# A fused attention and gated-MLP layer on one core: every product moved onto the two 64-row halves of the array

## The chip, the cores and the metric

One of the eight cores of a Trainium2 chip runs the whole layer. The time is the device time of one execution, in microseconds (us). TensorE (PE) does the matmuls and writes their sums to PSUM, which has eight banks of 512 float32 columns on 128 partitions; ScalarE (ACT), VectorE (DVE) and GpSimd (POOL) do the rest; SyncE (SP) issues all transfers. Every engine works through its own list of instructions in order, and the lists meet in semaphores.

## The reference

`x` is 2048 tokens by 448. 16 heads of 28; each query sees 8 keys, 2 tokens apart, itself the last.

```python
h  = x + A(layernorm(x));  h2 = h + B(layernorm(h))

def A(x, wqkv, wo):                       # 16 heads, Dh = 28
    q, k, v = split(x @ wqkv)
    logits = einsum('bhsd,bhswd->bhsw', q, k[:, :, s - 2*w]) * Dh**-0.5   # w = 0..7
    return (softmax(logits) @ v[:, :, s - 2*w]) @ wo

def B(x, w_in, w_sp, b_sp, w_out):
    z  = gelu(x @ w_in)                   # 448 -> 2 * 896
    z1, z2 = z[..., :896], layernorm(z[..., 896:])
    g  = einsum('ts,bsf->btf', w_sp, z2) + b_sp[None, :, None]            # 2048 x 2048
    return (z1 * g) @ w_out
```

## The kernel before, in words

Python builds a list of jobs, each with an engine, an estimated duration, what it reads and writes, and how many PSUM banks it takes. A planner (`Planner.order`) lays them out in simulated time; where several jobs of an engine are ready it takes the one with the lowest number in `PRIO`, a list with one rank per job. The result fixes each engine's order of instructions. Semaphore waits are then derived from the reads and writes (`Sched.issue`); PE never waits for itself, because its matmuls end in order. `ON` says which engine a PSUM evacuation or copy runs on.

**Products.** The contraction is over 448 rows: three chunks of 128 and one of 64. `product` (L554) makes two PE jobs for one pair of PSUM banks. Job F: six matmuls over 128 rows, three for each bank. Job H: two matmuls over the last 64 rows, one for each bank; the data of that chunk lie twice, on partitions 0 to 63 and 64 to 127, so that one runs on the upper and one on the lower half of the array (`tile_position` (0, 0) and (64, 0)). All of these matmuls are recorded at L564. Products are:

- `qk{t}_{g}`: queries and keys, for six blocks of tokens `t` (128, 128, 256, 512, 512, 512 tokens) and four groups `g` of four heads. One bank gets q, the other k of those heads, 28 rows for each head in a strip of 32; four rows of each strip hold zeros. Evacuated by `qe{t}_{g}` into `qkT` (L581), even and odd tokens apart.
- `v{b}`: values, for two attention blocks at a time (nine jobs), evacuated by `ve{b}` into `V1` (L575).
- `y{m}`: the projection with `wo`, two blocks of 128 tokens (eight).
- `z2_{m}` (sixteen) and `z1_{u}` (fourteen): the two halves of `w_in`, tokens on the partitions for z2, features for z1.

**Attention.** 17 blocks of up to 128 queries. `lg{b}_{j}` (L874) makes the logits of eight heads, with 28-row matmuls on 32-row strips: `j` = 0 uses strips 0 and 1, `j` = 1 strips 2 and 3. `ex` (ACT, L883) takes the exponential, `mk` (DVE, L889) masks it, `o{b}` (PE, L898, 16 matmuls over 128 rows) multiplies with the values and sums, `rc` and `om` (DVE, L906 and L909) divide. Then a transposing transfer, a copy into `OT`, `y`, the sum with x `h` (DVE, L843), the second layer norm (L696, L698, L691, L707), and a transposing transfer into `hnT`. `E` has four slots, so `lg{b}` waits for `o{b-4}`.

**Gated MLP.** z2 and z1 wait for the last logits (`gate`), since the GELU (L965, L1010) and the exponential use different ACT tables. A z2 product with a non-zero entry in `RAW2` is exempt: it may run earlier, is copied out raw (L575), and gets its GELU in place (L962). Then statistics (L969, L972) and normalisation (L978), the spatial product `g` (L1043, 448 matmuls of 512 columns over 128 rows), the gate `ua`, `um` (L1051, L1054), the output product (L1066), the sum (L1073), the store. A matmul of PE with nothing to do at the start is a filler (L1081).

**Changes of row use.** The planner charges PE for a change between full (F), half (H) and logit (L) jobs: `SWITCH`, about 0.1 us each.

Of the kernel before, what the change touches and what calls it, by code (L numbers as in the profile page):

```python
# [5 lines left out]
S_TOK = 2048  # L6
D = 448
NHEAD = 16
DH = 28
# [10 lines left out]
SWITCH = {"FH": 0.096, "HF": 0.096, "FL": 0.1, "HL": 0.1, "LF": 0.03, "LH": 0.1}  # L20
# [4 lines left out]
LOOK = {'pe': 1e-09, 'act': 0.1762690089245428, 'dve': 0.17500524126766434, 'pool': 0.04342214756282488, 'sp':  # L25
        0.3037332826506372}
PRIO = [0, 3, 4, 5, 1, 2, 14, 9, 7, 6, 10, 8, 13, 12, 11, 50, 58, 41, 38, 63, 62, 40, 54, 0, 0, 7, 16, 22, 34, 21, 15,
# [34 lines left out]
KEY = dict(x=-10.145, xs=0.685, qk=-3.702, qkg=-1.064, v=-1.761, ve=-6.148, qe=-3.15, lg=-1.488, ex=5.497,  # L62
           mk=-3.215, o=2.696, om=0.603, oT=-1.054, hh=0.0, y=-5.759, h=0.564, ln2=4.478, hT=19.942, z2=74.834,
           z2s=0.028, zr=2.556, zrs=0.21, z1=34.42, z1s=2.041, g=84.462, gs=0.172, wo=1.509, wl=-9.273,
           wls=4.361, wp=-9.955)
WINB = 2
ON = {'xe0_0': 'dve', 'xe0_1': 'act', 'xe1_0': 'dve', 'nd0_9': 'dve', 'nd0_10': 'dve', 'wp0_0': 'act', 'wp0_1': 'act',
# [41 lines left out]
class Sched:  # L109
# [14 lines left out]
    def issue(self, exe, fn, reads=(), writes=(), dma=False):  # L124
# [23 lines left out]
        for e, c in sorted(needed.items(), key=lambda t: -t[1]):  # L148
# [8 lines left out]
            if c > myvc.get(e, 0):  # L157
                myvc[e] = c
# [980 lines left out]
```

## Time and profile before

| | us |
|---|---|
| three runs | 242.96, 242.97, 242.81 (median 242.96) |
| the profiled execution | 243.6 |
| its span, first to last instruction | 241.9 |
| last logits start (the group on `qkL`) | 73.2 |
| first spatial matmul | 109.2 |
| last start of a z2 group | 121.0 |

A row of a timeline gives the start, the time from the first start to the last end, engine, line, operation, tiles, rows by columns of the array used, the shape of the moving operand, and how many instructions were merged. Matmuls overlap by their fill and drain, so the spacing of their starts tells the price, not their duration. PEld is the load of weights, which runs under the matmuls. In a table of windows the columns are the window, its length, then PE, PEld, DVE, ACT and POOL, each with busy time and the number of instructions, the granted PE clock, the share of the transfer engines and GB/s. In a table of groups the numbers behind the bar are the busy time in us, the mean duration of one in ns, and, behind the second bar, the idle time before them and what ended it.

### The profile page before, as it was taken

How to read it: one execution, taken by the hardware profiler on the slowest of the kernel's cores; microseconds unless marked ns; L12 is line 12 of the kernel's file. 1: busy time of each engine (PE TensorE's matmuls, PEld its weight loads, DVE VectorE, ACT ScalarE, POOL GpSimd, SP SyncE). 2: the span in 40 equal slices, each digit the busy share in tenths (PEclk: the TensorE clock that was granted, in tenths of full speed). 3: DMA queues.
4: the chain of work that ended last, by engine and by line, in shares of the span. 5: the costliest groups of instructions: out<-in, count | busy, mean ns of one | idle time of the engine just before them, and what ended most of it. 6: DMA issues, size and time to landing. Idle time of an engine off the chain costs nothing.

```text
span 241.9 us, 4239 instructions
## 1 busy us (share of the span) xinstructions
PE 235.4 (97%) x1707; PEld 115.5 (48%) x1726; DVE 155.0 (64%) x319; ACT 92.6 (38%) x115; POOL 55.4 (23%) x110
## 2 busy tenths in 40 slices
PE   7999999999999999999999999999999999999995
PEld 5674545545545444444344444444444444434443
DVE  6999878998999999998573135106111920805554
ACT  2779777778989765666230000000000000033000
POOL 8535116255565533061111000000000000000000
PEclk9999999999999999999999999999999999999999
DMA  6954497958533999999899400000000020010112
GB/s 194 317 138 94 77 157 176 171 133 190 109 62 72 176 152 179 228 158 153 166 204 178 42 0 0 0 3 0 0 0 3 0 76 0 20 41 0 57 38 76
DMA packets 65923, 23.21 MB, mean 96 GB/s; under 512 B 58352, under 2 KB 65648, under 8 KB 65904
## 3 DMA queue, kind: packets, MB, share of 16 engines
q1 hardware_dynamic: 65904, 22.95, 46.9%
q8 instruction: 13, 0.21, 0.4%
q14 instruction: 6, 0.05, 0.1%
HBM read 6.83 MB, written 1.84 MB: 36 GB/s over the span
## 4 chain that ended last, share of the span: by engine, by line
PE 92%; DMA 2%; DVE 2%; SPq 1%; issue 1%; ACT 0%; ACTq 0%
PE psum L1043 40%; PE psum L564 37%; PE psum L1066 9%; PE psum L874 3%; PE psum L898 3%; DMA wraw<-in_A_wqkv_dram 2%; DVE E L889 1%; SPq L605 1%; DVE qkT L581 1%; ACT wqk L575 0%; PE psum L738 0%; DVE srg L1073 0%; PE psum L740 0%; ACTq L179 0%
## 5 line engine op out<-in xcount | busy, mean ns | idle before, releaser
L1051 DVE TENSOR_TENSOR ub<-psum,bb 128x512 bf16<-128x512 f32 x28 | 19.4, 691 | 50.4 <-PE psum L1043 50.0
L1043 PE MATMUL psum<-wsp_hi,z2p 128*128 128x512 bf16 x217 | 50.6, 379 | 0.4
L1010 ACT ACTIVATE z1p<-psum 128x1024 bf16<-128x1024 f32 x14 | 14.1, 1021 | 95.8 <-PE psum L564 95.8
L1043 PEld LDWEIGHTS psum<-wsp_hi,z2p 128*128 128x128 bf16 x224 | 21.8, 98 | 26.2 <-issue 0.4
L883 ACT ACTIVATE E<-psum 128x960 bf16<-128x960 f32 (+2 forms) x34 | 31.7, 973 | 6.5 <-PE psum L874 6.4
L564 PE MATMUL psum<-xhT,wqk 128*128 128x512 bf16 (+5 forms) x185 | 27.6, 306 | 1.0 <-issue 0.5
L1043 PE MATMUL psum<-wsp_la,z2p 128*128 128x512 bf16 x110 | 26.0, 379 | 0.1
L1043 PE MATMUL psum<-wsp_lb,z2p 128*128 128x512 bf16 x109 | 25.6, 379 | 0.2
L564 PE MATMUL psum<-w_in,hnT 128*128 128x448 bf16 (+1 forms) x128 | 24.3, 353 | 0.1
L564 PE MATMUL psum<-hnT,w_in 128*128 128x512 bf16 (+1 forms) x112 | 23.9, 379 | 0.0
L1066 PE MATMUL psum<-w_out,z1p 128*128 128x448 bf16 (+1 forms) x119 | 22.8, 341 | 0.0
L969 DVE BATCH_NORM_STATS2 st<-z2p 128x6 f32<-128x448 bf16 x32 | 19.2, 612 | 4.2 <-ACT z2p L965 3.7
L889 DVE TENSOR_TENSOR E<-E,maskb 128x1920 bf16<-128x1920 bf16 (+2 forms) x17 | 20.3, 1220 | 1.0 <-ACT E L883 1.0
L696 DVE BATCH_NORM_STATS2 st<-x_tm 128x6 f32<-128x448 bf16 x32 | 19.0, 612 | 1.5 <-DMA x_tm<-in_A_x_dram 1.3
L691 POOL TENSOR_TENSOR rs<-rs,negh 128x2 f32<-128x2 f32 (+2 forms) x22 | 18.6, 847 | 1.8
L564 PEld LDWEIGHTS psum<-xhT,wqk 128*128 128x128 bf16 (+1 forms) x192 | 12.6, 97 | 11.3 <-issue 3.2
L1043 PEld LDWEIGHTS psum<-wsp_la,z2p 128*128 128x128 bf16 x112 | 10.9, 98 | 13.3 <-issue 0.4
L1054 DVE TENSOR_TENSOR z1p<-ub,z1p 128x512 bf16<-128x512 bf16 x28 | 11.9, 424 | 8.4 <-ACT z1p L1010 7.5
L1043 PEld LDWEIGHTS psum<-wsp_lb,z2p 128*128 128x128 bf16 x112 | 11.0, 98 | 13.1
L581 ACT ACTIVATE qkT<-psum 128x1024 bf16<-128x1024 f32 (+2 forms) x22 | 15.0, 717 | 4.8 <-PE psum L564 4.5
L1066 PEld LDWEIGHTS psum<-w_out,z1p 128*128 128x128 bf16 x119 | 11.6, 98 | 10.3
L564 PEld LDWEIGHTS psum<-w_in,hnT 128*128 128x128 bf16 (+1 forms) x128 | 10.1, 97 | 12.7 <-issue 4.1
(63 smaller groups left out, 241.8 us busy)
## 6 DMA issues: line engine op xcount, KB each, us to landing
w_in<-in_B_w_in_dram SPq DMA_DIRECT2D x8, 224.0 KB, 3.2
out_dram<-srg SPq DMA_DIRECT2D x16, 112.0 KB, 1.7
x_tm<-in_A_x_dram SPq DMA_DIRECT2D x3, 448.0 KB, 6.2
w_out<-in_B_w_out_dram SPq DMA_DIRECT2D x1, 784.0 KB, 8.2
wraw<-in_A_wqkv_dram SPq DMA_DIRECT2D x1, 672.0 KB, 5.4
bb<-in_B_b_sp_dram SPq DMA_DIRECT2D x1, 512.0 KB, 6.4
wo<-in_A_wo_dram SPq DMA_DIRECT2D x1, 336.0 KB, 6.0
wv<-in_A_wqkv_dram SPq DMA_DIRECT2D x1, 336.0 KB, 6.2
```

Source lines behind the costliest of these rows:

```text
L564: ins = e.matmul(o, w, x, start=g not in seen, stop=left[g] == 0, **kw)
L581: return e.activation(o, i, AF.Copy) if eng == "act" else e.tensor_copy(o, i)
L691: (lambda e: e.tensor_tensor(R, A, negh[:, 0:1].to_broadcast([128, n]), ALU.pow), [rr, r_negh], r_rs[k][m:m + n])],
L696: [(lambda e: e.bn_stats(st[:, m, :], src), [rsrc], [r_st[k][m]])], dve_t(D))
L883: return e.activation(o, i, AF.Exp, scale=SCALE)
L889: return e.tensor_tensor(a, a, maskb[:, mi:mi + 1, pad:pad + nq].to_broadcast([NK, NHEAD, nq]), ALU.mult)
L969: [(lambda e, m=m, k=k: e.bn_stats(st3[:, m, k, :], z2p[:, m, D * k:D * (k + 1)]), [r_z2[m]], [r_st[2][m]])], dve_t(D))
L1010: return e.activation(o, i, AF.Gelu_apprx_tanh)
L1043: ins = e.matmul(psv(tk), z2p[:, s, 128 * fc:128 * fc + 128], w, start=(s == 0), stop=(s == NB - 1))
L1051: [(lambda e, tc=tc, s=s, tk=tk: e.tensor_tensor(ub[:, s, :], psv(tk), bb[:, 512 * tc:512 * tc + 512], ALU.add), [r_bb], [r_ub[s]])], dve_ ...
L1054: [(lambda e, fc=fc, tc=tc, s=s: e.tensor_tensor(z1p[:, fc, 512 * tc:512 * tc + 512], ub[:, s, :], z1p[:, fc, 512 * tc:512 * tc + 512], AL ...
L1066: ins = e.matmul(psv(tk, 0, c1 - c0), z1p[:, fc, 128 * m:128 * m + 128], w_out[:, fc, c0:c1], start=(fc == 0), stop=(fc == FC7 - 1))
```

## The change

- `product` makes two jobs of another cut. Job A: for each of the three 128-row chunks the upper 64 rows go to one bank and the lower 64 rows to the other; then the two matmuls of the last chunk, as before. Job B: the three chunks again with the banks exchanged. All are half-row matmuls, 14 for each product in place of six full and two half. As B's halves write the banks that A's other halves wrote, B's first instruction waits until PE's own semaphore has counted A (`own`, `behind`). Block 16's values, alone in one bank, become four full matmuls (`single`).
- From block `t` = 3 on (`T7`, tokens 512 to 2047) the product for the last four heads has only q. Their k comes from the four spare rows of each strip in the other seven banks: four POOL copies (`wr0` to `wr3`) put the weights there before block 3, `qs{t}` makes q in two banks of half the columns, and four transfers for each block (`qr{t}_{j}`, four more for `qkL`) gather the rows into the place of k. The logits wait for them.
- The planner learns the costs of the new kinds: the two logit jobs of a block are told apart by row half (L and M), a wait of B costs 0.25 us (`SELF`).
- `PRIO`, `ON`, `LOOK`, `KEY`, `WLH` and `GRES` are other; `RAW2` is all zeros. `OH` (the `o` jobs on halves) is off: `fo2` is not used.

```diff
-SWITCH = {"FH": 0.096, "HF": 0.096, "FL": 0.1, "HL": 0.1, "LF": 0.03, "LH": 0.1}
+SWITCH = {"FH": 0.111, "HF": 0.098}
+OH = False
+SELF = 0.25
...
-RAW2 = [0, 1, 2, 1, 1, 1, 1, 2, 1, 2, 1, 0, 0, 1, 0, 0]
+RAW2 = [0] * 16
 XEH = {0: 2}
-WLH = [4, 4, 8, 9, 18, 1, 4, 12, 24, 4, 14, 34, 6, 22, 21, 26]
-GRES = 1
+WLH = [2, 3, 5, 6, 8, 9, 11, 12]
+GRES = 4
...
-ON = {'xe0_0': 'dve', 'xe0_1': 'act', 'xe1_0': 'dve', 'nd0_9': 'dve', 'nd0_10': 'dve', 'wp0_0': 'act', 'wp0_1': 'act',
-      'wp1_0': 'act', 'wp4_0': 'act', 'wp4_1': 'act', 'qe4_1': 'dve', 'qe4_3': 'dve', 'oc1': 'pool', 've2': 'dve', 'od3':
-      'dve', 'oc3': 'pool', 've4': 'dve', 'od4': 'dve', 'oc5': 'pool', 'od6': 'dve', 'od7': 'dve', 'oc7': 'pool', 'nd1_5':
-      'dve', 've8': 'dve', 'oc9': 'pool', 've10': 'dve', 'oc11': 'pool', 'oc13': 'pool', 'nd1_10': 'dve', 'oc15': 'pool',
-      'nd1_14': 'dve', 'nd1_15': 'dve', 'z2c6': 'dve', 'z2c13': 'dve'}
+ON = {'xe0_1': 'act', 'nd0_8': 'dve', 'nd0_10': 'dve', 'nd0_13': 'dve', 'nd0_15': 'dve', 'wp0_0': 'act', 'wp1_1': 'act',
+      'wp2_0': 'act', 'wp2_1': 'act', 'wp3_0': 'act', 'wp4_0': 'act', 'wp4_1': 'act', 'qe0_1': 'dve', 'qe2_3': 'dve', 'qe3_0':
+      'dve', 'qe3_3': 'dve', 'qe4_0': 'dve', 'qe4_2': 'dve', 'qe5_0': 'dve', 've0': 'dve', 'oc1': 'pool', 've2': 'dve', 'oc3':
+      'pool', 'od5': 'dve', 'oc5': 'pool', 'oc7': 'pool', 'nd1_4': 'dve', 'od9': 'dve', 'oc9': 'pool', 'nd1_6': 'dve',
+      'nd1_7': 'dve', 'oc11': 'pool', 'od13': 'dve', 'od15': 'dve', 'oc15': 'pool', 'nd1_12': 'dve', 'nd1_15': 'dve'}
...
+        if own > myvc.get("own", 0):
+            waits.append((exe, own))
+            myvc["own"] = own
...
             def f(e, which):
-                parts = get()
...
-                for g, o, w, x, tp in parts[which]:
-                    left[g] -= 1
-                    kw = {} if tp is None else {"tile_position": tp}
-                    ins = e.matmul(o, w, x, start=g not in seen, stop=left[g] == 0, **kw)
-                    seen.add(g)
+                main, rest = get()
+                seqs = [[q for q in main if q[0] == k] for k in range(2)]
+                nc = len(seqs[0])
+                assert nc == len(seqs[1])
+                for c in range(nc):
+                    for k in range(2):
+                        g, o, w, x, _ = seqs[k ^ which][c]
+                        i = 64 * k
+                        ins = e.matmul(o, w[i:i + 64], x[i:i + 64], start=which == 0 and c == 0, stop=which == 1 and c == nc - 1,
+                                       tile_position=(i, 0))
+                if which == 0:
+                    for k, (g, o, w, x, tp) in enumerate(rest):
+                        assert g == k and tp == (64 * k, 0)
+                        ins = e.matmul(o, w, x, start=False, stop=False, tile_position=tp)
                 return ins
...
+            jh = pl.job(name + "B", "pe", key + KEY["hh"], [(lambda e: f(e, 1), reads, [])], half_t(n) * nc, acq=tk, kind="H")
+            jh.behind = jf
...
+            for i in range(4 if t == T7 else 0):
+                pool("wr%d" % i, KEY["wp"] + 20.0 + i, [
+                    (lambda e, i=i: e.tensor_copy(
+                        wqk[:, :, 0:7, :].rearrange("p c g (j q) -> p c g j q", q=32)[:, :, :, :, DH + i],
+                        wraw[:, :, D + 336:2 * D].rearrange("p c (j q) -> p c j q", q=28)[:, :, :, 7 * i:7 * i + 7].rearrange(
+                            "p c j g -> p c g j")), W_qk, [r_pad3[i]])], 0.5)
+            for g in range(3 if t >= T7 else 4):
...
+            product("qs%d" % t, key, f, [r_pad[6]] + r_pad2 + r_pad3 + xh_res(lo, hi), n // 2, 6, tk)
...
+            for j in range(4):
+                load("qr%d_%d" % (t, j), lambda j=j, lo=lo, hi=hi: qkv(slice(7, 8), lo, hi)[32 * j:32 * j + DH, 0],
+                     lambda j=j, lo=lo, hi=hi: qkT[32 * j + DH:32 * j + 32].rearrange("p g (r t) -> p (g r) t", r=2)[:, 0:14, lo // 2:hi // 2],
+                     [r_qr[t][j]], 0.6, (1.4, 0.2), key=lo / 112.0 + KEY["qe"] + 1.0, reads=r_qk[t])
```

More of the change, by code (lines that the diff above doesn't have):

```diff
@@ L79 @@
 LN1G = [(0, 1), (1, 1), (2, 2), (4, 4), (8, 4), (12, 4)]
+T7 = 3
 QT = [(0, 128), (128, 256), (256, 512), (512, 1024), (1024, 1536), (1536, 2048)]
@@ L122, in __init__, with issue @@
         self.store_keys = []
-    def issue(self, exe, fn, reads=(), writes=(), dma=False):
+    def issue(self, exe, fn, reads=(), writes=(), dma=False, own=0):
         prod, inc = exe, 1
@@ L197 @@
     __slots__ = ("eng", "key", "dur", "lat", "ops", "acq", "rel", "tick", "reserve",
-                 "deps", "ndep", "succ", "idx", "start", "end", "name", "tbl", "srv", "kind", "alts")
+                 "deps", "ndep", "succ", "idx", "start", "end", "name", "tbl", "srv", "kind", "alts", "behind", "done")
 class Planner:
@@ L219, in job @@
         j.alts = None
+        j.behind = None
+        j.done = 0
         deps = set(a for a in after if a is not None)
@@ L341, in order @@
             if e == "pe":
[L342 to L346 removed]
+                was, now = pstate[0], j.kind
+                if was.upper() in "LM" and now in "LM":
+                    if was.upper() != now and t < te[e] + 0.05:
+                        dur -= 0.1
+                        now = now.lower()
+                elif now in "LM":
+                    dur += 0.1
+                elif was in "LM":
+                    dur += 0.1
+                elif was in "lm":
+                    dur += 0.03
+                elif was != now:
+                    dur += SWITCH[was + now]
+                pstate[0] = now
             j.start = t
@@ L364, in order @@
                 s.ndep -= 1
-                a = j.end + (lat if s.eng != "pe" else 0.0 if e == "pe" else lat + FILL)
+                a = j.end + (lat if s.eng != "pe" else lat + FILL if e != "pe" else SELF if s.behind is not None else 0.0)
                 avail[s] = max(avail.get(s, 0.0), a)
@@ L812, in values @@
             lo, hi = k0s[0], k0s[-1] + sd * (NK - 1) + 1
-            product("v%d" % b, key, f, W_v + xh_res(lo, hi), D, 3 * nb, tk, [o_jobs.get(b + i - NV) for i in range(nb)])
+            product("v%d" % b, key, f, W_v + xh_res(lo, hi), D, 3 * nb, tk, [o_jobs.get(b + i - NV) for i in range(nb)], single=nb == 1)
             sl = b % NV
@@ L865, in bass_sequential_preLN__sliding_local_dilated__mixer_gmlp__prompt_kernel @@
                     rq += r_qk[t] if sd == 2 else r_qkL
+            rr = [[], []]
+            for t, (lo, hi) in enumerate(QT):
+                if t >= T7 and lo < t0 + sd * nq and hi > t0 - sd * pad:
+                    for j in range(2):
+                        rr[j] += (r_qr[t] if sd == 2 else r_qrL)[2 * j:2 * j + 2]
             for j in range(2):
@@ L901, in fo, with fo2 @@
                 return ins
-            o_jobs[b] = pl.job("o%d" % b, "pe", b + KEY["o"], [(fo, [r_E[slot], r_V[vs]] + r_Eh[slot], [])], 0.40, acq=tk)
-            rsl, os = b % 4, b % NO
+            def fo2(e, nq=nq, slot=slot, vs=vs, tk=tk):
+                for h in range(8):
+                    for k, i in ((0, 0), (1, 64), (1, 0), (0, 64)):
+                        hd = 8 * k + h
+                        ei = 4 * (hd % 4) + hd // 4
+                        ins = e.matmul(psum[:, (tk.b + k) * 512 + 32 * h:(tk.b + k) * 512 + 32 * h + DH + 1],
+                                       E[i:i + 64, slot, ei * nq:ei * nq + 128], V1[i:i + 64, vs, hd, 0:DH + 1],
+                                       start=h == 0 and i == 64 * k, stop=h == 7 and i == 64 - 64 * k, tile_position=(i, 0))
+                return ins
@@ new lines, in bass_sequential_preLN__sliding_local_dilated__mixer_gmlp__prompt_kernel, with heads @@
+            o_jobs[b] = pl.job("o%d" % b, "pe", b + KEY["o"], [(fo2 if OH else fo, [r_E[slot], r_V[vs]] + r_Eh[slot], [])], 0.40, acq=tk,
+                               kind="H" if OH else "F")
+            rsl, os = b % 4, b % NO
+            def heads(nq, tk):
+                if OH:
+                    return psum[0:nq, tk.b * 512:tk.b * 512 + 1024].rearrange("p (k n) -> p k n", k=2)[:, :, 0:256].rearrange(
+                        "p k (h d) -> p k h d", d=32)
+                return psv(tk, 0, 512, nq).rearrange("p (k h d) -> p k h d", k=2, d=32)
@@ L1095, in bass_sequential_preLN__sliding_local_dilated__mixer_gmlp__prompt_kernel @@
                     reads += brs
-                key = sch.issue(j.eng, fn, reads, writes, dma=len(op) > 3)
+                key = sch.issue(j.eng, fn, reads, writes, dma=len(op) > 3, own=j.behind.done if j.behind is not None else 0)
+                j.done = sch.cnt[key]
                 if j.name.startswith("out"):
```

84 lines of the change are left out of this document (51 added, 33 removed), and 69 rows, old and new, of the table PRIO.

## The prediction

> **What bounds the kernel now.** I read the page's busy times first, then the chain of waits, then the windows by stage, then the timeline of single groups of matmuls.
>
> ```profile
> PE 235.4 (97%) x1707; PEld 115.5 (48%) x1726; DVE 155.0 (64%) x319; ACT 92.6 (38%) x115; POOL 55.4 (23%) x110
> PEclk9999999999999999999999999999999999999999
> PE 92%; DMA 2%; DVE 2%; SPq 1%; issue 1%; ACT 0%; ACTq 0%
> 20.00:40.00 20.00, 19.19 (x247) 9.53 (x250) 17.66 (x31) 16.71 (x19) 6.94 (x12) 1.00 0.65 114
> 40.00:60.00 20.00, 19.52 (x238) 10.06 (x238) 17.61 (x33) 15.32 (x20) 9.25 (x12) 1.00 0.87 174
> 60.00:73.20 13.20, 13.05 (x168) 6.70 (x169) 12.65 (x23) 11.76 (x15) 7.93 (x13) 1.00 0.49 96
> 73.20:110.00 36.80, 36.75 (x269) 16.95 (x270) 35.23 (x82) 26.70 (x30) 15.08 (x31) 1.00 0.86 157
> ```
>
> TensorE (PE) is busy 97% of the span, at a granted clock of 0.9 or more in every slice, and makes 92% of the chain. Outside the first 10 us it hardly waits, so what counts is how many microseconds of PE work there are and whether PE stays fed. The windows (length, then PE, PEld, DVE, ACT, POOL) add a warning: VectorE (DVE) is busy 88% from 20 to 60 us and 96% from 60 to 110. It is the second bound of the attention part, a few per cent behind PE.
>
> "Busy" hides what PE loses inside its stream. The starts of single groups show that:
>
> ```profile
> 97.75 3.38 PE L564 MATMUL psum<-w_in,hnT 128*128 128x448 bf16 x17
> 84.83 0.35 PE L564 MATMUL psum<-wo,OT 128*128 128x448 bf16 x1
> 85.11 0.36 PE L564 MATMUL psum<-wo,OT 64*128 64x448 bf16 x2
> 85.31 0.73 PE L564 MATMUL psum<-w_in,hnT 64*128 64x448 bf16 x6
> 85.98 0.36 PE L564 MATMUL psum<-w_in,hnT 128*128 128x448 bf16 x1
> ```
>
> Seventeen full matmuls take 3.38 us, the last of them 0.35: 16 spacings of 0.189. The six half matmuls (three pairs, each pair on both halves of the array) take 0.73, the last 0.35: two spacings of 0.19. So a pair of halves streams exactly as fast as one full matmul, with its own weights loaded underneath. But from the last full start (84.83) to the first pair it is 0.28, and from the last pair's start (85.31 + 2 x 0.19 = 85.69) to the next full matmul 0.29: each change between 128-row and 64-row use costs about 0.10. With the slower second step after it (the pair at 85.31 starts 0.20 after that at 85.11, not 0.19) I take 0.107.
>
> **The change part by part.**
>
> *Streaming time of the products.* Six full matmuls and one pair become seven pairs: at equal spacing nothing is gained or lost.
>
> *Changes of row use.*
>
> ```profile
> 9.80 0.34 PE L564 MATMUL psum<-xhT,wqk 64*128 64x128 bf16 x6 [0.19 <-ACT wqk L575]
> 215.24 3.29 PE L564 MATMUL psum<-hnT,w_in 128*128 128x512 bf16 x16
> ```
>
> Going through the matmuls in order of time, from the first half group (9.80 us) to the last z1 units (from 215.24 us, halves among them), I count 46 changes between full and half, and 42 into or out of the logit groups (L874, 28 rows): 88 x 0.107 = 9.4 us. After the change the 46 go. But `o` (L898) stays full, and each run of it now stands between half-row jobs. The logits stay too, and z1 or z2 products set between the spatial matmuls (L1043) now pay twice per visit. If all 17 `o` jobs stand beside a logit group: some 36 changes; if nothing is joined (21 logit runs and 15 runs of `o` as now): 72; plus 10 for five visits among L1043, as there are now. I take 66, nearer the upper end because the groups stand apart today: 22 x 0.107 = 2.3 us saved (bounds 0.6 and 4.5).
>
> *Logit groups.* They are told apart by their row half in the new ranking (kinds L and M). The chain shows what two jobs in a row cost:
>
> ```profile
> 53.02 0.34 PE psum L874 x16
> 60.98 0.53 PE psum L874 x16
> ```
>
> Same 16 matmuls, 0.34 or 0.53: where the two jobs use different halves they overlap. Six runs of 16 cost 0.5 or more, and eight jobs stand alone; joining them saves up to 6 x 0.19 + 4 x 0.2 = 1.9. I take 1.2 (bounds 0 and 1.9).
>
> *Last four heads' k.* For the last three token blocks of 512 one product of two banks by 512 columns becomes one of two banks by 256.
>
> ```profile
> L564 PE MATMUL psum<-xhT,wqk 128*128 128x512 bf16 x65 | 16.4, 380 | 0.8 <-issue 0.5 <-ACT qkT L581 0.2
> L564 PE MATMUL psum<-xhT,wqk 128*128 128x256 bf16 x24 | 3.3, 274 | 0.0
> 30.77 0.24 POOL L575 COPY xn<-xn 128x64 bf16<-128x64 bf16 x1
> ```
>
> The mean falls by 0.106 per slot, since fill and drain stay: 7 slots x 3 blocks x 0.106 = 2.2 us of PE. Evacuation of those falls too, hidden. Four POOL copies (112 elements each) stand before the third block's products; a POOL copy of 64 takes 0.24, so I put them at 4 x 0.4 = 1.6 us, hidden behind the value products that run before that block. Sixteen SP transfers are new, between the evacuation and the logits:
>
> ```profile
> 30.86 1.02 ACT L581 ACTIVATE qkT<-psum 128x1024 bf16<-128x1024 f32 x1 [0.59 <-PE psum L564]
> 32.45 0.41 PE L874 MATMUL psum<-qkT 28*128 28x120 bf16 x16
> out_dram<-srg SPq DMA_DIRECT2D x16, 112.0 KB, 1.7
> OTs<-otm SPq DMA_TRANSPOSE x8, 3.2
> ```
>
> The block's last evacuation ends at 31.88, its first logits start at 32.45. A transfer of 28 KB has no row; the nearest land 1.7 us (plain) and 3.2 us (transposing, same queue) after issue, so the logits come 1.1 to 2.6 later, less 0.7 of shorter product. PE has the next block's products meanwhile, but the exponentials and masks behind those logits start later. I take 0.7 us of loss (bounds 0 and 2.6). For the two later blocks `qk` can be ranked ahead.
>
> *The wait on PE's own semaphore.* Job B writes the banks that job A's other half wrote, so it waits for A to end. No row shows PE waiting for itself; the nearest is PE waiting for DVE:
>
> ```profile
> 36.43 3.31 DVE L889 TENSOR_TENSOR E<-E,maskb 128x1920 bf16<-128x1920 bf16 x2
> 39.80 0.56 PE L898 MATMUL psum<-V,E 128*128 128x29 bf16 x16 [0.48 <-DVE E L889]
> ```
>
> DVE ends at 39.74, PE starts at 39.80: 0.06. A's last matmul lasts 0.35 and would have let the next start after 0.19, so a bare wait costs 0.35 + 0.06 - 0.19 = 0.22 us. Queued behind it on PE is everything else, and the evacuation of that product. There are 70 products (12 + 12 for q and k, 8 values, 8 projections, 16 z2, 14 z1): all bare 15.4 us, none bare 0. Cover is any job of another product (at least 3 slots of 0.19) or a logit or `o` job between A and B. Each product still takes two banks, so eight banks allow four at once. I take 5 bare ones' worth, 1.1 us; they will be found at the start and where banks are short.
>
> *Ranks anew, and no early z2.* RAW2 is now all zero, so no z2 product may run before the last logits; the kernel before has these ahead of the last logits at 73.16:
>
> ```profile
> 67.63 1.78 PE L564 MATMUL psum<-w_in,hnT 128*128 128x448 bf16 x10
> 69.66 1.60 PE L564 MATMUL psum<-w_in,hnT 128*128 128x448 bf16 x8
> 73.16 0.40 PE L874 MATMUL psum<-qkL 28*128 28x112 bf16 x16
> L575 ACT ACTIVATE z2p<-psum x9: 909/917/918, 69.3 to 110.0; 128x896 bf16<-128x896 f32 x9
> ```
>
> Three z2 products (the third starts at 71.51), some 4.0 us of PE, go behind the last logits. The nine ACT copies of 0.92 vanish; ACT is at 77 to 89% there and off the chain, so that buys room only. With 4.0 moved, 2.2 of k saved and about 2 of switches and logits, PE's work before the last logits ends at 73.2 - 8.2 = 65.0. Can DVE be there by then? To 73.2 it was busy 64.7 (16.81 for the first 20 us, and the rows above) and idle 8.5. Of this the second layer norm can be put off:
>
> ```profile
> 0.00:20.00 20.00, 18.25 (x186) 12.56 (x187) 16.81 (x50) 11.96 (x25) 12.36 (x38) 1.00 0.74 204
> L696 DVE BATCH_NORM_STATS2 st<-x_tm 128x6 f32<-128x448 bf16 x24 | 14.1, 611 | 1.4 <-DMA x_tm<-in_A_x_dram 1.3
> L707 DVE TENSOR_SCALAR xn<-x_tm,mv,rs 128x448 bf16<-128x448 bf16 x22 | 8.8, 431 | 0.9 <-POOL rs L691 0.9
> L843 DVE TENSOR_TENSOR x_tm<-psum,x_tm 128x896 bf16<-128x896 f32 x4 | 4.3, 1086 | 0.0
> L698 DVE BATCH_NORM_AGGREGATE mv<-st 128x2 f32<-128x6 f32 x24 | 3.2, 163 | 0.2
> L575 DVE CAST V<-psum 128x896 bf16<-128x896 f32 x4 | 4.4, 1092 | 1.5 <-PE psum L564 1.5
> L581 DVE CAST qkT<-psum 128x1024 bf16<-128x1024 f32 x2 | 2.4, 1224 | 1.0 <-PE psum L564 1.0
> L575 DVE CAST xhT<-psum 128x512 bf16<-128x512 f32 x1 | 0.7, 677 | 0.0
> L575 DVE CAST xhT<-psum 128x256 bf16<-128x256 f32 x1 | 0.4, 424 | 0.2 <-PE psum L740 0.2
> ```
>
> Eight of the 24 statistics (4.9) and aggregates (1.3), six of the 22 normalisations (2.6) and the four sums (4.3) are its share: 13.1. The new table puts seven q/k evacuations on DVE for two (four of 1024 elements, two of 512, one of 256, and one rest of 256: by these rows 4 x 1.22 + 2 x 0.68 + 2 x 0.42 = 7.1 for 2.4) and two value evacuations for four (2.2 less): +2.5. So DVE's floor is 64.7 - 13.1 + 2.5 + 8.5 = 62.6, under PE's 65.0 by 2.4. But what is put off is missing right after, when PE wants z2. I take the last logits 1.5 us past 65.0, as PE idle, nearer the floor than today's 73.2; bounds 0 and 8.2.
>
> *Sum:* -2.3 - 1.2 - 2.2 + 0.7 + 1.1 + 1.5 = -2.4 us of span: 241.9 to 239.5. The profiled execution took 243.6 with this span of 241.9; the runs shown have a median of 242.96, 0.6 under it. The difference goes onto the median: **240.6 us**.
>
> **Rivals.**
>
> *Attention starves PE (the slower side).* The place is PE's stretch before the last logits, now without z2 as filler; the price is 1 us for each microsecond that these come after 65.0. The other terms make -3.9, so it decides from 68.9 us on. With the logits as late as today the sum is -3.9 + 8.2 = +4.3: 247.3. For it: DVE at 88 to 96%, more evacuations on it, and the key transfer at 32 us. Against: 13.1 us of DVE work that can wait, and only 2.5 come in.
>
> *Bare waits.* If B mostly stands right behind A, at a half of 70 it is 7.7 instead of 1.1: 247.2; all of them, 254.9. For it: banks, two per product, held until both jobs and the evacuation are done. Against: cover of 0.6 us from any other product's job, and products are plentiful at nearly all times.
>
> *Loads as the bound.* Each product has 14 weight loads for 8.
>
> ```profile
> L564 PEld LDWEIGHTS psum<-xhT,wqk 128*128 128x128 bf16 (+1 forms) x192 | 12.6, 97 | 11.3 <-issue 3.2
> L564 PE MATMUL psum<-xhT,wqk 64*128 64x128 bf16 x16 | 1.0, 219 | 0.2 <-ACT wqk L575 0.2
> ```
>
> Two loads of 97 ns, one after the other, are 194 per pair: 5 over 189 in 224 pairs of 448 columns, 85 over 109 in 49 of 256, 138 over 56 in 56 of 128: +13.0 us, 253.6. Against it stands the row at 9.80: three pairs of 128 columns in 0.34, the last 0.22, so 0.06 apart. The two loads of a pair overlap.
>
> The Trainium skill (TensorE: Matmul & The Clock Gate, LDWEIGHTS (loading the stationary operand)) says that a load's time goes by its columns and not its rows, 128 at 1.2 GHz, so a half load costs a whole one. By that figure two in a row would be an estimated 213 ns and the loss 19 us. The trace agrees on the price of one load (97 against 107) but not that they queue.
>
> *It cancels*, with 2 us more idle than I take.
>
> **How the numbers follow.** PE-bound with the sum as above, 237.5 to 242.4: 0.58. Cancelled, within 0.2% (0.5 us, about what a measurement of this kernel tells from no change): 0.08. Starved PE 0.19, bare waits 0.10, loads 0.02, the key transfers late in all three blocks 0.03: slower 0.34. Range: downward the better bounds of switches and logits and no idle or bare waits (-2.2 - 4.5 - 1.9 = -8.6 at best; two thirds of it, 236.8), upward to 246.5, which holds most of the starved case: about 0.1 is left out on each side.
>
> **What would show it.** Right: only four full matmuls left in the products, pairs of halves 0.19 apart; in the windows PE over 97% from 20 to 110; last logits (qkL) at 65 to 68 us; the spatial matmuls in one piece from about 126. Wrong: PE waiting for PE at over 2 us in all; qkL past 69; PE idle on ACT or DMA between 30 and 36; pairs of 448 columns 0.2 apart or more.

## The result, and the profile after

The changed kernel takes **252.21 us** (median of 4 runs, 250.96 to 253.3), the kernel before 242.97 beside it: a ratio of 1.038, with a 95% interval of 1.031 to 1.044. The forecast was 240.6, in a range of 236.8 to 246.5. The profiled execution took 253.26 us with a span of 251.5.

The page of the changed kernel, busy times, granted clock and shares of the chain:

```profile
PE 240.0 (95%) x2153; PEld 119.6 (48%) x2153; DVE 153.6 (61%) x320; ACT 84.1 (33%) x107; POOL 53.8 (21%) x110
...
PEclk9999997999858999999999999999999999999999
...
PE 76%; DVE 4%; ACT 3%; DMA 3%; SPq 2%; issue 0%
```

PE's share of the chain has fallen from 92% to 76%. That alone does not show the loss: it is 76% as well in the run without the key move below, which takes 244.35 us. The clock row says more: all nines before, it has two dents now. The windows say where (length, then PE, PEld, DVE, ACT, POOL, and the clock as the last but two):

```profile
20.00:40.00 20.00, 17.35 (x262) 9.04 (x259) 16.48 (x30) 12.48 (x15) 7.74 (x14) 1.00 0.36 65
40.00:60.00 20.00, 19.88 (x310) 10.09 (x309) 16.31 (x25) 15.87 (x21) 8.18 (x10) 0.91 0.82 135
60.00:75.00 15.00, 12.10 (x160) 5.81 (x160) 10.65 (x22) 9.48 (x12) 7.50 (x13) 0.74 0.80 153
75.00:110.00 35.00, 34.84 (x416) 17.44 (x414) 32.28 (x75) 20.81 (x24) 10.70 (x23) 0.96 0.87 135
```

PE lacks 2.65 us between 20 and 40 and 2.9 between 60 and 75, and each time the clock sinks afterwards: "busy" then counts microseconds at less than full speed. What PE waited for (total, times, longest):

```profile
PE psum L945 <- DMA qkT<-qkT: 4.5, 3, 1.9
PE psum L770 <- DVE xn L739: 1.6, 2, 1.2
```

L945 are the logits, and the new transfers of the keys hold them up. The chain of waits through the first of the three places, where the block's four transfers (SPq L637) were issued from 33.12 on (the last one from 35.47; it lands at 39.45):

```profile
34.78 0.65 SPq L637
35.43 0.04 issue
35.47 3.98 DMA qkT<-qkT
39.45 0.14 issue
39.59 0.39 PE psum L945 x8
```

and PE's timeline there and at the other two places (start, length, then in brackets idle time before it):

```profile
37.42 0.39 PE L945 MATMUL psum<-qkT 28*128 28x120 bf16 x8 [0.38 <-issue]
39.59 0.39 PE L945 MATMUL psum<-qkT 28*128 28x120 bf16 x8 [1.78 <-DMA qkT<-qkT]
39.90 0.60 PE L969 MATMUL psum<-V,E 128*128 128x29 bf16 x16
40.44 2.74 PE L590 MATMUL psum<-xhT,wqk 64*128 64x512 bf16 x12
42.97 0.60 PE L595 MATMUL psum<-xhT,wqk 64*128 64x512 bf16 x2
43.50 0.41 PE L945 MATMUL psum<-qkT 28*128 28x120 bf16 x16
43.84 0.82 PE L590 MATMUL psum<-xhT,wqk 64*128 64x512 bf16 x6
...
66.30 0.38 PE L945 MATMUL psum<-qkT 28*128 28x120 bf16 x8 [1.87 <-DMA qkT<-qkT]
67.58 0.58 PE L945 MATMUL psum<-qkT 28*128 28x120 bf16 x8 [0.90 <-DMA qkT<-qkT]
...
80.66 0.40 PE L945 MATMUL psum<-qkL 28*128 28x112 bf16 x16
```

Read the lengths as well as the waits. Six pairs and the first start of the next, from 40.44 to 42.97, are 0.42 us apart; the three pairs at 43.84 last 0.82, that is two spacings of 0.22 and the last matmul's 0.38. The same pairs of 512 columns run at half speed in the first place. The windows around the two places:

```profile
36.00:40.00 4.00, 1.84 (x42) 1.11 (x39) 1.84 (x3) 1.07 (x2) 0.24 (x1) 1.00 0.51 76
40.00:43.40 3.40, 3.40 (x30) 1.27 (x29) 2.11 (x3) 0.97 (x1) 0.54 (x2) 0.50 1.12 139
63.30:67.30 4.00, 1.51 (x24) 0.68 (x22) 2.98 (x3) 2.65 (x4) 1.01 (x1) 1.00 0.95 102
67.30:77.50 10.20, 9.91 (x108) 4.49 (x110) 6.60 (x13) 6.66 (x9) 5.09 (x9) 0.50 0.91 166
```

After 4 us in which PE was busy 1.84, it ran 3.4 us (40.0 to 43.4) at half clock; after 4 us with 1.51, it did so for 10.2 us (67.3 to 77.5). So a wait is paid twice here, once as idle time and once more in the stretch behind it. The last logits start at 80.66.

How fast do four key transfers move? The DMA view of the changed kernel from 34 to 39 us, in 40 slices of 0.125 us (busy tenths of the 16 engines, then GB/s):

```profile
DMA  0000011211212122212121222211158889344969
GB/s 0 0 0 0 4 33 25 25 20 20 29 20 29 21 29 25 25 20 29 20 25 20 41 74 82 45 29 25 25 82 154 152 176 135 55 68 74 80 39 45
```

Alone from about 34.6 to 36.8 us they occupy 0.1 to 0.2 of the engines, two or three of 16, and move some 25 GB/s. Four of 28 KB are 114,688 bytes, 4.6 us at that rate. The Trainium skill (DMA: Bandwidth & Descriptors, Why a DMA increments its semaphore by 16 and not by 1) gives the rule: a transfer runs on the largest number of engines, at most 16, that divides the slowest dimension on both sides. Here these are 4 partitions at the source and 28 at the destination, so four; in the trace each of these transfers lands in five events (the skipped engines' share at once, then four), the loads to 128 rows in 16. The trace agrees. That the number of engines sets the 25 GB/s, and not the form of their packets, no run tests.

### The profile page after: what moved, and what is told of

Same layout as the page of the kernel before. It is cut to its first block, busy times and chain, and to the rows that moved or that the text cites. A ratio compares the mean times of both kernels' runs of the same rounds, so it can differ in the third digit from the quotient of the medians.

```text
span 251.5 us, 5125 instructions
## 1 busy us (share of the span) xinstructions
PE 240.0 (95%) x2153; PEld 119.6 (48%) x2153; DVE 153.6 (61%) x320; ACT 84.1 (33%) x107; POOL 53.8 (21%) x110
## 3 DMA queue, kind: packets, MB, share of 16 engines
HBM read 6.83 MB, written 1.84 MB: 34 GB/s over the span
## 4 chain that ended last, share of the span: by engine, by line
PE 76%; DVE 4%; ACT 3%; DMA 3%; SPq 2%; issue 0%
PE psum L1131 39%; PE psum L590 22%; PE psum L1154 8%; PE psum L595 4%; DMA qkT<-qkT 3%; DVE E L960 2%; PE psum L945 2%; ACT E L954 2%; PE psum L969 2%; SPq L637 1%; DVE qkT L613 1%; ACT qkT L613 1%; ACT V L607 1%; PE psum L577 1%; SPq L636 1%; DVE x_tm L909 0%
## 5 line engine op out<-in xcount | busy, mean ns | idle before, releaser
L1131 PE MATMUL psum<-wsp_hi,z2p 128*128 128x512 bf16 x224 | 51.6, 379 | 0.0
L954 ACT ACTIVATE E<-psum 128x960 bf16<-128x960 f32 (+2 forms) x34 | 32.8, 985 | 15.9 <-PE psum L945 15.8
L590 PE MATMUL psum<-xhT,wqk 64*128 64x512 bf16 (+2 forms) x288 | 24.8, 303 | 0.5 <-DVE V L607 0.3
L1131 PE MATMUL psum<-wsp_la,z2p 128*128 128x512 bf16 x112 | 25.0, 379 | 0.0
L590 PE MATMUL psum<-w_in,hnT 64*128 64x448 bf16 x192 | 22.8, 349 | 0.2 <-DVE rcp L994 0.2
L590 PE MATMUL psum<-hnT,w_in 64*128 64x512 bf16 x168 | 21.6, 376 | 0.0
L1053 ACT ACTIVATE z2p<-psum 128x896 bf16<-128x896 f32 x16 | 14.2, 918 | 13.6 <-PE psum L590 13.6
L1161 DVE TENSOR_TENSOR srg<-psum,x_tm 128x448 bf16<-128x448 f32 (+1 forms) x17 | 9.9, 594 | 11.1 <-PE psum L1154 8.9
L1154 PEld LDWEIGHTS psum<-w_out,z1p 128*128 128x128 bf16 x119 | 11.6, 98 | 10.2
L945 PE MATMUL psum<-qkT 28*128 28x120 bf16 (+1 forms) x256 | 11.3, 229 | 4.9 <-DMA qkT<-qkT 4.5
L590 PEld LDWEIGHTS psum<-xhT,wqk 64*128 64x128 bf16 x288 | 11.5, 96 | 8.1 <-issue 0.8
```

Source lines behind the costliest of these rows:

```text
L590: ins = e.matmul(o, w[i:i + 64], x[i:i + 64], start=which == 0 and c == 0, stop=which == 1 and c == nc - 1, tile_position=(i, 0))
L945: ins = e.matmul(psum[:, c:c + nq], src[p:p + DH, 2 * g + 1, q0 - pad:q0 - pad + NK], src[p:p + DH, 2 * g, q0:q0 + nq], start=True, stop=True,
L954: return e.activation(o, i, AF.Exp, scale=SCALE)
L1053: pl.job("z2g%d" % m, "act", kz, [(lambda e, o=out2, i=in2: e.activation(o(), i(), AF.Gelu_apprx_tanh), [], [r_z2[m]])], act_t(FH), use=[t ...
L1131: ins = e.matmul(psv(tk), z2p[:, s, 128 * fc:128 * fc + 128], w, start=(s == 0), stop=(s == NB - 1))
L1154: ins = e.matmul(psv(tk, 0, c1 - c0), z1p[:, fc, 128 * m:128 * m + 128], w_out[:, fc, c0:c1], start=(fc == 0), stop=(fc == FC7 - 1))
```

## The experiments

Where a run is said to have a fixed order, each engine takes its jobs strictly in a given list; this is the edit for it, and the ranks are then that list:

```diff
+        line = {e: sorted(j.key for j in self.jobs if j.eng == e and j is not self.filler) for e in self.ENGS}
+        gone = set()
...
+                head = next((k for k in line[e] if k not in gone), None)
                 for j in ready[e]:
+                    if j is not self.filler and j.key != head:
+                        continue
```

**Without the key move.** The changed kernel in its own order, all heads' k by full products again:

```diff
-T7 = 3
+T7 = 6
```

> The changed kernel without the move of the last four heads' k: these come from a full product again, there are no key transfers and no wr copies, and every engine keeps the changed kernel's order. Theory 1 (the logits wait for the key transfers, PE idles, and its clock then drops to half): both waits and both half-clock stretches vanish, clock 1.00; 9 us less, plus 2.2 us of k products: 242 to 245. Theory 2 (the halves themselves cost: pairs slower than full matmuls, or bare waits of PE on itself): still 250 or more, with the clock as it comes.

Measured: 244.35 us, ratio 1.005 (1.003 to 1.007). Its windows, and its longest waits of PE after the start's:

```profile
20.00:40.00 20.00, 20.00 (x312) 10.24 (x308) 17.01 (x33) 13.42 (x17) 5.19 (x11) 1.00 0.45 75
40.00:60.00 20.00, 20.00 (x322) 10.10 (x322) 17.51 (x31) 17.61 (x22) 8.99 (x11) 1.00 0.70 149
60.00:80.00 20.00, 18.94 (x312) 10.16 (x312) 18.66 (x37) 16.87 (x19) 10.75 (x17) 1.00 0.90 148
```

PE is full from 20 to 60 at full clock. Theory 1 held. The key move, meant to save 2.2 us, costs 252.21 - 244.35 = **7.9 us**; halves, waits and ranks together cost 1.2 (the kernel before took 243.19 beside this run).

**The same with PE kept busy.** The changed kernel in its order, with 23 matmuls whose result is overwritten put ahead of the three waiting logits:

```diff
+KW = {(4, 0): 9, (13, 0): 10, (13, 1): 4}
...
+                if (b, j) in KW:
+                    def fk(e, n=KW[b, j], tk=tk):
+                        for _ in range(n):
+                            ins = e.matmul(psv(tk, 0, D), xhT[:, 0, 0:128], wv[:, 0, :], start=True, stop=True)
+                        return ins
```

> The changed kernel with extra matmuls without use ahead of three logit jobs that wait for key transfers: 9 before lg4_0, 10 before lg13_0, 4 before lg13_1 (0.19 us each, into a bank that the logits overwrite). The transfers are awaited as before. Theory 1, with the clock as its larger half: no half-clock stretch, 245 to 248. Rival 1b (only the waits matter, the clock costs nothing since PE idles anyway): 251 to 254, whatever the clock is. Rival 1c (the clock drops for another reason than idling): half-clock stretches stay.

Measured: 249.64 us, ratio 1.024 (1.021 to 1.027), clock 1.000. Its timeline at the first place, and the longest of its waits:

```profile
37.39 1.88 PE L966 MATMUL psum<-wv,xhT 128*128 128x448 bf16 x9
39.46 0.38 PE L959 MATMUL psum<-qkT 28*128 28x120 bf16 x8 [0.20 <-DMA qkT<-qkT]
```

```profile
PE psum L604 <- DMA hnT<-xn: 1.7, 1, 1.7
```

The transfers are as late as ever, but PE stays at full clock, and 252.21 - 249.64 = 2.6 us come back with no useful work added. So it is the idling that brings the half clock here. The time lies between the ranges of theory 1 (245 to 248) and rival 1b (251 to 254), so the full clock gave less back than theory 1 asked: 1.7 us go again further on, where PE, now earlier, waits for the normalized rows `hnT`.

**Halves without the rest.** The kernel before, in its own order held fixed, with its products on the halves by the changed `product` function:

```diff
-            left, seen = {}, set()
...
+                main, rest = get()
+                seqs = [[q for q in main if q[0] == k] for k in range(2)]
...
+            jh.behind = jf
```

> The kernel before with its products on halves alone (jobs A and B in the places of F and H, whichever came first), k products whole, ranks and tables of before as a fixed order. 16 of 70 B jobs stand directly behind their A. Theory 1: streaming is unchanged, the bare waits cost 16 x 0.22 = 3.5 us and o now changes row use: 244 to 248, clock 1.00. Theory 2 (halves are the cause of the loss): 250 or more.

Measured: 248.25 us, ratio 1.019 (1.017 to 1.021), just above the range of theory 1. In this order 16 of the 70 jobs B stand directly behind their A. One of them, its A's last pair first:

```profile
88.67 0.35 PE L596 MATMUL psum<-wo,OT 64*128 64x448 bf16 x2
89.08 0.74 PE L591 MATMUL psum<-wo,OT 64*128 64x448 bf16 x6
```

0.41 us from start to start where a pair takes 0.19: a bare wait costs 0.22, the price forecast. Sixteen make 3.5 of the 5.1 us by which this run is slower than the kernel before beside it (243.19); the other 1.6 were not taken apart. An order made for the two jobs is a part of the change that it can't do without.

**The key move without the rest.** The kernel before, in its order held fixed, with the moved keys alone:

```diff
+T7 = 3
-            for g in range(4):
+            for g in range(3 if t >= T7 else 4):
...
+            for j in range(4):
+                load("qr%d_%d" % (t, j), lambda j=j, lo=lo, hi=hi: qkv(slice(7, 8), lo, hi)[32 * j:32 * j + DH, 0],
```

> The kernel before with the move of k alone: full and half products as before, qs and the transfers from block 3 on, ranks of before as a fixed order, transfers issued right after the block's last evacuation. Theory 1: the first logits of each block come 3 to 5 us later, and this order has nothing else to run meanwhile: 248 to 256, with half-clock stretches. Theory 2: about 241 to 244, since 2.2 us of products are saved and the transfers are hidden.

Measured: 267.04 us, ratio 1.093 (1.086 to 1.100), above the 256 at which even theory 1 ended; clock of the profiled run (268.22, the longest of four) 0.942. PE's wait:

```profile
PE psum L930 <- DMA qkT<-qkT: 18.1, 3, 10.1
```

An order that knows nothing of the transfers pays all of their delay, up to 10.1 us at once.

**Later readers.** The changed kernel, its order made with a landing time of the key transfers as its trace shows it, then held fixed; on PE the first logits that need moved keys stand behind a product of the next block. Only the list differs:

```diff
-PRIO = [9, 7, 3, 4, 0, 1, 15, 12, 13, 2, 8, 10, 16, 14, 18,
+PRIO = [25, 17, 11, 13, 0, 4, 46, 30, 36, 8, 21, 26, 48, 40, 54,
...
```

> The changed kernel with all its parts, instructions and transfers; only the order on the engines is another. It was made with a longer time for the key transfers, the one that the trace of the changed kernel shows (the first lands some 2.6 us after its issue ends, each further one of a block 1.25 us later), and is then held fixed: on PE the logits that read moved keys stand behind other products, and come later. Theory: the loss is not in the move itself but in where its readers stand; with them behind other work PE does not wait for the transfers (4.5 us of waits gone or under 1 us), so its clock does not fall either (1.00 instead of 0.973), and the time goes to 241.5 to 244.5 us, ratio 0.994 to 1.006. Rival 1: the transfers take the longer, the later they are issued, or the logits cannot stand later without the attention behind them waiting for ACT: PE waits elsewhere for as long, 247 us or more. Rival 2: moved keys need more than they save even where nothing waits, then it is no faster than the kernel with the move taken out (244.4 us).

Measured: 250.81 us, ratio 1.031 (1.026 to 1.035). Rival 1 held. No wait on the key transfers is left; in its place, by the list of waits and by the chain:

```profile
PE psum L603 <- DMA xhT<-xn: 2.8, 1, 2.8
```

```profile
35.83 5.38 DMA xhT<-xn
```

At 41.2 the transposing transfer lands that feeds the next block's product; it is issued behind the four key transfers and takes 5.4 us. The delay has moved from their readers to a transfer that runs beside them, and PE idles even longer at the same place (2.8 us for 1.8): the clock of that execution is 0.980. It is not the place in SP's queue that makes it late. The same transfer takes 2.4 us in the run without the key move (first row here), and still 4.8 us in the run further down that has the four on POOL's queue and the same order (second row):

```profile
DMA to landing us min/median/max: 2.4/2.4/2.4
```

```profile
DMA to landing us min/median/max: 4.8/4.8/4.8
```

**Two queues.** The changed kernel in its order, held fixed, two of a block's four transfers issued by POOL:

```diff
-                     [r_qr[t][j]], 0.6, (1.4, 0.2), key=lo / 112.0 + KEY["qe"] + 1.0, reads=r_qk[t])
+                     [r_qr[t][j]], 0.6, (1.4, 0.2), key=lo / 112.0 + KEY["qe"] + 1.0, reads=r_qk[t], eng="pool" if j in (1, 2) else "sp")
```

> The changed kernel in its own order, held fixed; of the four key transfers of each block two are issued by POOL instead of SP. It asks what makes them late: theory: the few DMA engines that all four use (4 of 16, 23 to 26 GB/s in sum). Then the second queue changes little: the last of the four still lands some 4.5 to 6 us after the first issue begins, and the time stays within 1.5 us of the changed kernel (250.7 to 253.7 us). Rival: the issues on SP, 0.65 to 0.88 us each and one behind the other, and the order within one queue set the pace; with two queues side by side the last lands 1.5 to 2.5 us earlier, PE's two waits shrink by as much, the clock falls less, and the time is 246 to 249 us.

Measured: 246.68 us, ratio 1.014 (1.006 to 1.023). PE's only wait on key transfers, and around it the chain (first POOL issue of the block at 31.65):

```profile
PE psum L958 <- DMA qkT<-qkT: 1.1, 1, 1.1
```

```profile
33.01 4.67 DMA qkT<-qkT
```

The landing times are the theory's: the last is there at 33.01 + 4.67 = 37.68, 6.0 us after the first issue, for 6.3 in the changed kernel, so a second queue does not make four such transfers faster. The time is the rival's, and for another reason than it gave. In the first block the wait is shorter (1.1 us for 1.8). In the last one the four issues now start between 56.09 and 57.0 us, where in the changed kernel a transposing transfer on SP stood between them (60.06 to 63.67), and no wait is left there. That is enough to reach the edge of the clock. The four executions are the clearest picture of the second price. Two kept a clock of 1.000 and took 244.10 and 244.99 us; two had 0.986 and 0.979 and took 248.38 and 248.82. The same instructions, 4 us apart, and the mean clock tells them apart: PE fell to half clock or it didn't. How often can be read from the mean. A stretch of 3.41 us at half clock loses 1.7 us, 0.007 of such an execution, and the traces agree: one stretch goes with 0.993 (later readers with four on POOL), three in all with 0.980 (later readers), four with 0.973 (the changed kernel). So 0.986 and 0.979 are two and three, an estimate of 3.4 and 5.1 us; where they lie is not shown, since these two executions have no trace. At full clock the move with two queues takes what the kernel takes without it (244.35): it then pays for itself and gains nothing.

**Two queues and new orders.** Two orders searched for with the landing times so far seen, held fixed. Edit: the list of ranks, on top of the edit above.

> All parts of the change, with the key transfers issued by SP and POOL, two each, as in the run before with two queues, and with the order on all engines made anew for the landing times that the traces show, then held fixed: on PE the first logits that read moved keys stand some 2 to 3 us further behind the transfers than in the changed kernel, and other products stand ahead of them. Theory: the loss was late transfers and the half clock that follows; with cover for both, PE waits for transfers under 1 us in all, the clock is 1.00 in every execution, and what is left of the change's gains shows: 241 to 243.5 us, ratio 0.992 to 1.002. Rival: other transfers behind the key transfers on SP (those that transpose the normalized rows) are late in turn, as in the run with the later order, and PE waits for these and falls to half clock: 247 us or more.

> The same as the run before it, with another order made for the same landing times, in which the logits of the fourth and fifth block stand a little later still on PE and the normalized rows are transposed at other points. Theory: as there, 241 to 244 us with a clock of 1.00. If the two orders differ by more than 2 us, then it is not the key transfers alone that decide, but what each order puts behind them on SP.

Measured: 253.80 us (1.043, 1.038 to 1.049) and 252.99 us (1.040, 1.033 to 1.047). Both missed. In the first, PE waits for no key transfer, but:

```profile
PE psum L603 <- issue: 2.9, 1, 2.9
PE psum L1182 <- DVE warm L705: 2.1, 1, 2.1
PE psum L783 <- DVE xn L752: 1.7, 1, 1.7
PE psum L603 <- DMA xhT<-xn: 1.3, 1, 1.3
PE psum L603 <- POOL rs L735: 1.2, 1, 1.2
```

An order tuned to one corrected time leans on all the others. Here PE waits for the normalized rows instead, their statistics (POOL rs), DVE's own step (xn) and the transfer that transposes them (xhT). The longest wait, 2.9 us ahead of a product with `wo`, names no releaser ("issue"), and 2.1 us belong to the start (1.5 in the other runs).

**All four on POOL, and the later readers with it.** The edit with the two queues, for all of `j` in the first and second run and for two in the third; the second and third in the order of the later readers.

> The changed kernel in its own order, held fixed; all four key transfers of each block are issued by POOL, none by SP. Theory A: transfers of this form from SP's queue all lie on the same four DMA engines, one behind the other, while those from POOL's queue go to other engines in turn. Then the four land 2.5 to 4 us after their own issues, the last one at most 4 us behind the last issue, none of the transposing transfers on SP's queue stands behind them, and PE's wait for them is at most that of the run with two and two (1.1 us): 243.5 to 246.5 us, clock 1.00 in most executions. Theory B: all such transfers share four engines from either queue, or POOL's slower issues (0.75 to 0.95 us each) eat the gain: the last lands as late as in the changed kernel, waits of 2 us or more, half clock, 248 us or more.

> The run with the later logits again, with one thing other: all four key transfers of each block are issued by POOL. There PE waited 2.8 us for a transposing transfer of the normalized rows that stood behind the key transfers on SP's queue (5.4 us from its issue to its landing), and fell to half clock. Theory A: with the key transfers gone from SP's queue that transfer lands in 2.5 to 4.5 us, PE waits for it under 1 us, the clock is 1.00, and with the logits placed late enough for the keys no wait over 1 us is left in the attention: 241.5 to 244 us. Theory B: the transposing transfer is late for another reason, or the value copies on POOL are late behind the issues: 247 us or more.

> The same with two of the four key transfers on POOL and two on SP. Theory A: between the two: the transposing transfer stands behind two key transfers instead of four, waits shrink by about half, 242 to 247 us. Theory B: as with four on POOL, no better than the later order by itself (250.8 us).

Measured: 249.12 us (1.020, 1.013 to 1.027), 248.82 (1.024, 1.019 to 1.030) and 247.64 (1.014, 1.009 to 1.018). Times to landing of the first block's transfers on POOL's queue, with two there (the two queues above) and with four, and what PE waited for most in the second, the start's wait aside:

```profile
DMA to landing us min/median/max: 3.4/3.5/3.5
```

```profile
DMA to landing us min/median/max: 3.5/4.7/5.0
```

```profile
PE psum L958 <- issue: 2.4, 2, 2.2
PE psum L783 <- DVE xn L752: 1.9, 2, 1.6
```

Theory A fell for four on POOL: they hold each other up there too (3.5 to 5.0 us, against 3.4 to 3.5 for two), and the first block's logits wait 1.47 and 0.72 us, 2.2 in all, where 1.1 was the most that theory A allowed. In the second run the wait for `xhT` is gone, but that transfer still takes 4.8 us (theory A: 2.5 to 4.5), and the logits wait 2.15 us at 39.09, with "issue" as releaser, which names no transfer. The key transfers fit: the second of the four, issued at 33.3, takes 5.7 us and so lands at 39.0. The third run, with 0.3 us left of the wait for `xhT` (2.8 with all four on SP), is as forecast in kind and just above its range, yet no faster than the change's own order with two queues. Their executions part by the clock again: 246.63 at 1.000 and 251.96 at 0.973 in the first, for one. The trace of the execution with 246.63 also shows that idle time does not always cost the clock. Its 4 us at the first place are as empty as those of the changed kernel (1.84), and PE stays at full clock:

```profile
36.00:40.00 4.00, 1.81 (x52) 1.47 (x52) 1.34 (x3) 1.43 (x2) 0.24 (x1) 1.00 1.00 120
```

No version beat the kernel before.

## Why the prediction was wrong

**The step that failed** is the term for the key transfers: "I take 0.7 us of loss (bounds 0 and 2.6)". That the logits come later was right; its size was not, nor that PE has other work until then. The bounds came from transfers with 1.7 and 3.2 us to landing, rows of transfers that do not share this form. The four land from 36.4 to 39.45, the last one 6.3 us after the first issue: they share some 25 GB/s, 4.6 us for the four, and a second queue saved 0.3 of the 6.3. Nothing in the trace before gave that number, but the shape (4 partitions to 28) was in the diff, and no bound was taken from it. With -2.2 for the shorter product, move and transfers were put at -1.5; they measured +7.9: 9.4 us of the error.

Two things behind this step were not in the sum at all. "PE has the next block's products meanwhile" holds for 4.7 us from the first issue; at 37.8 PE runs out, and the transfers need 6.3. And a wait was priced at its own length. By the run with the fillers, the half clock behind it costs another 2.6 us net; by the executions with two queues it is 4. Gross it is more: the four stretches of 3.41 us at half clock lose 6.8 us. An estimate from these rows is 4.5 of waits + 6.8 of clock - 2.2 of shorter products = 9.1, where the spans of the two profiles (251.5 and 243.5) are 8.0 apart; the first product, which comes 1.0 earlier with the move (11.16 for 12.15), may be the rest. "For the two later blocks `qk` can be ranked ahead" held for the first of them, where PE does not wait, but not for the last: its waits are 1.87 and 0.90. Of the rivals, "the key transfers late in all three blocks" is the one that came nearest (late in two of three), and it had 0.03, without a price. One slip in the range changes nothing: two thirds of 8.6 are 5.7, so its lower end should be 237.2 and not 236.8.

**The other terms.** Without the key move the steps give 242.96 - 2.3 - 1.2 + 1.1 + 1.5 = 242.1, and 244.35 was measured: 2.3 us too low. Together with the 9.4 that is the whole miss.

- *Changes of row use:* 88 to 66 forecast. Counting full, half and logit matmuls over the whole run there are 90 before and 72 after: 18 x 0.107 = 1.9 us instead of 2.3, an estimate, since no run changed this alone. Near enough.
- *Streaming:* pairs of halves run as full matmuls do. The timeline of the changed kernel has three pairs in 0.73, two spacings of 0.19 and a last 0.35:

```profile
95.57 0.73 PE L590 MATMUL psum<-w_in,hnT 64*128 64x448 bf16 x6
...
134.30 1.04 PE L1131 MATMUL psum<-wsp_lb,z2p 128*128 128x512 bf16 x4
```

  The rival of the weight loads is out: the two loads of a pair do not queue. The price of one load, for which the prediction names the Trainium skill (TensorE: Matmul & The Clock Gate, LDWEIGHTS (loading the stationary operand)), is not touched by that. The spatial matmuls do run on from 134.30, later than the 126 forecast by about what was lost before.
- *Bare waits:* the price of 0.22 was exact, their number was not: no job B stands directly behind its A in the changed order. In the starts of single matmuls three such waits show, some 0.13 us in all, against 1.1.
- *Last logits:* forecast 65 to 68, now 80.66, past the 68.9 from which "attention starves PE" should decide. But that rival put it down to DVE, and DVE is busy only 16.3 to 16.5 us of 20 there. Without the key move they start at 72.3 with PE full from 20 to 60 and 1.06 us idle from 60 to 80, where that rival's price, 1 us for each microsecond past 65.0, asks for 7.3. So lateness by itself costs little.
- *The start* was not a term, and should have been. The new ranks load `x` and the weights in another order, and job A needs every copy of the weights. The first product, at 8.22 before, comes at 11.16, and at 12.15 without the key move. The timelines of before and of the run without the key move:

```profile
8.22 1.28 PE L564 MATMUL psum<-xhT,wqk 128*128 128x128 bf16 x18
```

```profile
11.61 0.61 PE L1181 MATMUL psum<-warm 128*128 128x256 bf16 x4
12.15 0.34 PE L602 MATMUL psum<-xhT,wqk 64*128 64x128 bf16 x6
```

  In the meantime PE ran fillers (L1181; L1169 in the changed kernel). This lies nearest to the missing 2.3 us, but no run changed the start alone: what it costs net is open, and so is how the logit groups' 1.2 came out.

## What to carry to other kernels

Before a transfer takes over work of an engine, look at its shape on both sides, not its bytes: how many engines can share it, and what else is in flight beside it, on whatever queue. Price a wait of PE by what it can do to the clock as well: a stretch of about 2 us idle in 4 was paid again in the next 3 to 10 us in some executions and not in others, so a kernel near that edge has more than one time, here 4 us apart. A part of a change that saves little (2.2 us here) and adds a new dependency is best timed alone first; here it cost more than all other parts together could give.

## What the runs showed of the hardware

- A transfer from 4 partitions to 28 ran on four engines; four of them together moved 25 GB/s, and a transposing transfer issued behind them took 5.4 us from the start of its issue to its landing, still 4.8 with the four on another queue, and 2.4 without them. Two queues, or POOL's alone, did not speed up the four as a whole.
- The half clock came after 1.84 and 1.51 us of work in 4 and lasted 3.4 and 10.2 us, one and three times 3.41. What decides is open: with 1.81 in 4 (all four on POOL) it did not come, nor after a wait of 2.9 us in the first of the new orders. The Trainium skill (TensorE: Matmul & The Clock Gate, Part 1: The HAM clock gate) has such windows of about 3.4 us, and an idle one as the condition. The lengths agree with the trace. The condition is looser here: in the first place no gap is longer than 1.78 us, and PE still fell to half clock.
- A wait of PE on its own semaphore costs the last matmul's length plus 0.06 us: 0.41 from start to start at 448 columns (0.35 + 0.06), in the run with halves alone.
